# Top-k attention with two feed-forward layers: scores evicted over two PSUM banks at once for batch 0 and the batches made ahead

## The chip, the cores and the metric

One core of a Trainium2 chip runs the whole program. The metric is device time in microseconds (us). The kernel before was timed three times; the median is 1215.92 us.

## What is computed

The reference, cut to what matters (B, H, S, D are 4, 8, 576 and 64, top_k is 32, and x has 2304 rows of 512):

```python
scores = q @ k.transpose(0, 1, 3, 2) / np.sqrt(D)
kth = np.partition(scores, -top_k, axis=-1)[..., -top_k:-top_k + 1]
scores = np.where(scores >= kth, scores, -1e9)
attn = np.exp(scores - scores.max(-1, keepdims=True))
attn = attn / (attn.sum(-1, keepdims=True) + 1e-9)
x = (attn @ v).transpose(0, 2, 1, 3).reshape(B * S, H * D)
h = np.maximum(x @ w_in, 0.0)          # layer 1, d_ff = 2048
x = h * h @ w_out
h = x @ w2_in                          # layer 2
out = np.maximum(0.01 * h, h) @ w2_out
```

## The kernel before

**Tiles and pairs.** Attention is cut into 144 tiles of 128 rows of queries by 576 keys, in the order of `UNITS`: first the 36 tiles of batch 0 (tiles 0 to 35), then batch 1 and the rest. Two tiles make a pair; pairs 0 to 17 are batch 0. For each tile:

- `scores` multiplies on PE, in two halves of 288 keys (L279), each half into a PSUM bank of its own, and ACT copies each half to SBUF (L280). A tile takes 4 matmuls, or 8 where it crosses from one head to the other.
- DVE finds the 32 largest in each row: four MAX8 (L834) and three MATCH_REPLACE8 (L836), seven instructions a tile. The two tiles of a pair alternate, and the scheduler interleaves neighbouring pairs.
- POOL makes two constants of the pair from the maxima (`kf`, L291); ACT runs a Relu over each tile with them (L298), POOL subtracts (L299), ACT runs Exp with a row sum (L303), POOL and DVE make the reciprocal (L307, L308).
- PE transposes the tile (L317, L330), ACT evicts it to `PT` (L325, L343), PE multiplies by V (L401), DVE scales (`xn`, L432), and ACT and POOL split the result into a high and a low part (`xh` L433, `xl` L436), which is the input of the layers.

**Batches made ahead.** The scores of batches 2 and 3 (`EARLY`, 72 tiles) are made during pairs 0 to 15: matmul into tag `sp`, eviction to a `stage` tile, and a DMA to DRAM (`sd<-stage`, L283). They are read back when their turn comes (L287). Batch 0's scores go through tag `sd`, and batch 1's through the general banks `att`.

**PSUM until the layers start.** Three banks for `att`, two for `sd` (batch 0), three for `sp` (made ahead): eight. `sd` and `sp` rotate apart from each other. When the first block of 512 rows is ready, `open_mlp` gives their banks to the layers (`h`, one bank, and `acc`, four).

**The layers** run on PE in blocks (L580, L623, L625); ACT, DVE and POOL turn the weights into high and low parts (L513 to L526) and evict. The first block needs `xh` and `xl` of all four pairs of heads of its 512 rows. After that, work on the layers is interleaved with the attention of later pairs.

**What sets the order.** Each step is emitted at a slot (16 to a pair), and a scheduler then puts every engine's instructions into one fixed order, which is run strictly in that order. Tiles rotate through their buffers in the order of emission. Six score buffers (`s0` to `s5`, tile number modulo 6) and four `e` buffers are shared by all tiles.

Of the kernel before, what the change touches and what calls it, by code (L numbers as in the profile page):

```python
# [8 lines left out]
F = mybir.dt.float32  # L9
R = mybir.dt.float32r  # L10
U = mybir.dt.uint32
AF = mybir.ActivationFunctionType
# [31 lines left out]
FILL = (2, 245)  # L44
KPB = 2
NST = 3
SDB = 2
SPB = 3

NS = 6  # L50
NE = 4
# [20 lines left out]
def topk_attention_moe_moe2_kernel(  # L72
# [12 lines left out]
    P = 128  # L85
    DM, NF = 2 * NHP * D, w1.shape[0]
    NK = DM // P
    HALF = S // 2
# [5 lines left out]
    PE, ACT, DVE, POOL, SP = nc.tensor, nc.scalar, nc.vector, nc.gpsimd, nc.sync  # L94
# [6 lines left out]
    def bank():  # L101
        return psum.tile([P, 512], F, tag="att", name="att", bufs=3)
# [25 lines left out]
    for u in units:  # L128
        for hp in range(NHP):
            n = u["n"]  # L130
            uh = dict(u=u, hp=hp, n=n, b=u["b"], first=(u["t0"] == 0), ti=len(tiles), idx=len(uhs),
                      c0=P * (hp % 2) if n == 64 else 0)
# [14 lines left out]
    def direct(uh):  # L147
        return uh["b"] not in EARLY
# [10 lines left out]
    stage_psum = ahead_ctx.enter_context(tc.tile_pool(name="stage_psum", bufs=1, space=bass.MemoryType.PSUM))  # L159
    qsets = []  # L160
    for i in range(4):
        x = const if i < 2 else ahead
# [98 lines left out]
    def scores(t, half):  # L261
        uh = t["uh"]
        d = uh["qs"]
        kt = KT[uh["b"], uh["hp"]]
        if half == 0:
            if direct(uh):
                t["s"] = sbufs[t["i"] % NS]
            else:
                t["s"] = ahead.tile([P, S], F, tag="stage", name="stage", bufs=NST)
        ks = slice(half * HALF, (half + 1) * HALF)  # L270
        mm = [(x[:, h, c:c + P], kt[:, h, ks]) for h, c in t["parts"] for x in d]
        if not direct(uh):
            ps = stage_psum.tile([P, 512], F, tag="sp", name="sp", bufs=SPB)
        elif uh["b"] == 0:
            ps = stage_psum.tile([P, 512], F, tag="sd", name="sd", bufs=SDB)
        else:
            ps = bank()
        for i, (l, r) in enumerate(mm):
            PE.matmul(ps[:, 0:HALF], lhsT=l, rhs=r, start=i == 0, stop=i == len(mm) - 1)  # L279
        ACT.activation(t["s"][:, ks], ps[:, 0:HALF], AF.Copy)  # L280
        if half == 1 and not direct(uh):
            t["sd"] = dram.tile([P, S], F, tag=f"sd{t['i']}", name=f"sd{t['i']}")
            SP.dma_start(t["sd"], t["s"])  # L283
# [375 lines left out]
    for uh in uhs:  # L659
        b, hp, i = uh["b"], uh["hp"], uh.get("di")  # L660
# [50 lines left out]
    for n, key in enumerate(keys):  # L711
        ks = [(0, load_k, (*key, held[key]))]
        for h in range(2):
            ks.append((0, split_k, (*key, held[key], h)))
        if n == 0:
            fill += ks
        later = []
        for uh in later_uhs[key]:
            later += [(0, split_q, (uh, c)) for c in range(2)] + [(0, request, ())]
            for t in tiles[uh["ti"]:uh["last"] + 1]:  # L720
                later += [(1, scores, (t, half)) for half in range(2)]
        if n + 1 < len(keys):
            nk = keys[n + 1]
            ks = [(0, load_k, (*nk, held[nk]))]
            for h in range(2):
                ks.append((0, split_k, (*nk, held[nk], h)))
            m = len(later) // (len(ks) + 1)
            for x, item in enumerate(ks):
                later.insert((x + 1) * (m + 1) - 1, item)
        fill += later  # L730
# [9 lines left out]
    for p in range(NPAIRS):  # L740
        pr = dict(t=tiles[2 * p:2 * p + 2], p=p)
        pairs.append(pr)
        z = 16 * p
        for i, t in enumerate(pr["t"]):
            if direct(t["uh"]):
                at(z - DLEAD + 5 * i, scores, t, 0)
                at(z - DLEAD + 2 + 5 * i, scores, t, 1)
            else:
                at(z - LEAD + i, load_s, t)
            if i == 0:  # L750
                at(z + 14, shifts, pr)
            at(z + 14 + i, drop, pr, i)
            at(z + 16 + i, expo_sum, pr, i)
            if split(t["uh"]):
                at(z + 20 + i, norm, pr, i)
            at(max(z + 20 + 3 * i, z + 21 + i), pt_main, t)
        at(z + 18, recip, pr)
        at(z + 26, pt_left, pr)
# [60 lines left out]
    while slot <= last:  # L819
        p, i = divmod(slot, 16)  # L820
        if slot >= 0 and p < NPAIRS:
# [7 lines left out]
            x = i % 2  # L829
            t = pr["t"][x]  # L830
# [79 lines left out]
```

## Time and profile before

| | us |
|---|---|
| runs: lowest, median, highest | 1211.27, 1215.92, 1216.74 |
| span of the profiled execution | 1212.2 |
| PE busy | 1139.7 |
| DVE busy | 945.4 |
| ACT busy | 877.0 |
| POOL busy | 791.0 |

The span is 0.9 us above the lowest run and 3.7 below the median. The page gives no time outside the span, so the sum below is made on the span and then set on the median by those 3.7 us.

To read the views: a table by stretch gives, for each engine, busy time and, in brackets, the count of instructions in that stretch. In a timeline a row is start, duration, engine, line, operation, output<-input and count; where a row has x2, its duration covers both. The brackets at the end of a row are the time that the engine sat idle just before it, and who ended that.

### The profile page before, as it was taken

The page shows a single profiled execution, that of the slowest core. Times are in us where ns is not written, and L with a number is a line of the kernel's source. Part 1 is how long each engine was busy: PE and PEld are TensorE (multiplying, and loading weights), DVE is VectorE, ACT ScalarE, POOL GpSimd, SP SyncE. Part 2 cuts the span into 40 slices and gives each one's busy share as a digit, 9 for nine tenths or more (in the row PEclk, how much of TensorE's full clock was granted, in tenths as well). Part 3 has the DMA queues.
Part 4 walks back from the last instruction along what each step waited for, and adds up shares of the span by engine and source line. Part 5 has one row for each costly group of instructions (what it writes and reads, how often), then busy time and mean ns, then how long its engine had stood idle before and what let it go on. Part 6 is the DMA issues. An engine that isn't in the chain of part 4 may idle for free.

```text
span 1212.2 us, 20368 instructions
## 1 busy us (share of the span) xinstructions
PE 1139.7 (94%) x6388; PEld 994.3 (82%) x6388; DVE 945.4 (78%) x1944; ACT 877.0 (72%) x1939; POOL 791.0 (65%) x948
## 2 busy tenths in 40 slices
PE   5898878998899999999999999999999999999998
PEld 4676766886677879988998898788788899999997
DVE  7999999668888899999999999999999910110122
ACT  6889899888899997877767777676777763334322
POOL 7998977877889886667777685666576754004300
PEclk9899997999999999999999999999999999999999
DMA  9665656879889888889988788667576579779974
GB/s 308 230 226 194 196 196 245 268 252 315 306 292 343 296 279 272 301 289 367 349 294 286 256 280 285 202 229 233 193 232 223 197 261 374 255 254 339 359 251 137
DMA packets 110521, 323.24 MB, mean 267 GB/s; under 512 B 17488, under 2 KB 25680, under 8 KB 110416
## 3 DMA queue, kind: packets, MB, share of 16 engines
q1 hardware_dynamic: 107776, 317.24, 77.1%
q10 hardware_dynamic: 2640, 4.72, 1.1%
q8 instruction: 51, 0.84, 0.3%
q14 instruction: 54, 0.44, 0.1%
HBM read 254.54 MB, written 67.37 MB: 266 GB/s over the span
## 4 chain that ended last, share of the span: by engine, by line
PE 67%; ACT 10%; DVE 9%; DMA 3%; issue 2%; POOL 1%; ACTq 0%; SPq 0%; POOLq 0%
PE h L580 28%; PE acc L623 14%; PE acc L625 13%; DVE m L834 4%; PE att L412 3%; DVE w L836 3%; PE att L317 3%; DMA wraw<-in_w_dram 2%; PE att L401 2%; ACT e L303 2%; PE att L279 1%; ACT att L514 1%; ACT stage L280 1%; DVE PTs L323 1%; ACT s L280 1%
## 5 line engine op out<-in xcount | busy, mean ns | idle before, releaser
L580 PE MATMUL h<-xh,wi 128*128 128x512 f32 (+2 forms) x1280 | 350.0, 345 | 9.1 <-ACT wi L523 3.9
L834 DVE MAX8 m<-w 128x8 f32<-128x576 f32 x432 | 312.7, 748 | 1.5
L580 PEld LDWEIGHTS h<-xh,wi 128*128 128x128 f32 x1280 | 226.8, 190 | 38.6 <-ACT wi L523 4.3
L299 POOL TENSOR_TENSOR e<-s,e 128x576 f32<-128x576 f32 x144 | 203.4, 1431 | 26.6 <-ACT e L298 25.4
L836 DVE MATCH_REPLACE8 w<-m,w 128x576 f32<-128x576 f32 x288 | 213.2, 743 | 0.5
L580 PE MATMUL h<-xl,wi 128*128 128x512 f32 (+2 forms) x640 | 206.5, 340 | 1.4 <-DVE xl L637 1.1
L606 POOL TENSOR_TENSOR gl<-ga,gh 128x512 fp32r<-128x512 f32 (+2 forms) x160 | 162.8, 1017 | 38.1 <-ACT gh L605 32.5
L623 PE MATMUL acc<-gh,wo 128*128 128x512 f32 (+2 forms) x768 | 155.1, 340 | 0.0
L625 PE MATMUL acc<-wo,gh 128*128 128x512 f32 x576 | 151.5, 398 | 3.0 <-ACT gh L605 3.0
L603 POOL TENSOR_TENSOR ga<-ga,gb 128x512 f32<-128x512 f32 (+2 forms) x80 | 81.3, 1017 | 107.6 <-ACT gb L602 105.4
L623 PEld LDWEIGHTS acc<-gh,wo 128*128 128x128 f32 x768 | 125.9, 188 | 10.8 <-ACT gh L591 0.4
L580 PEld LDWEIGHTS h<-xl,wi 128*128 128x128 f32 x640 | 120.4, 189 | 14.7 <-DVE xl L637 4.0
L303 ACT ACTIVATE e<-e,kf 128x576 f32<-128x576 f32 x144 | 112.5, 782 | 17.3 <-POOL e L299 17.0
L625 PEld LDWEIGHTS acc<-wo,gh 128*128 128x128 f32 x576 | 103.9, 188 | 23.2 <-ACT gh L605 4.7
L298 ACT ACTIVATE e<-s,kf 128x576 f32<-128x576 f32 x144 | 105.7, 778 | 22.4 <-POOL kf L291 20.3
L834 DVE MAX8 m<-s 128x8 f32<-128x576 f32 x144 | 104.7, 748 | 13.4 <-ACT s L280 12.4
L592 POOL TENSOR_TENSOR ga<-ga 128x512 f32<-128x512 f32 (+2 forms) x80 | 66.2, 828 | 68.2 <-ACT gh L591 66.0
L836 DVE MATCH_REPLACE8 w<-m,s 128x576 f32<-128x576 f32 x144 | 107.0, 743 | 0.6
L317 PE MATMUL att<-ident,e 128*128 128x128 f32 x576 | 89.4, 284 | 13.0 <-ACT e L303 7.5
L312 ACT ACTIVATE e<-e,rc 128x576 f32<-128x576 f32 x108 | 78.0, 773 | 21.3 <-DVE rc L308 21.1
L317 PEld LDWEIGHTS att<-ident,e 128*128 128x128 f32 x576 | 69.8, 145 | 26.6 <-ACT e L303 12.8
L623 PE MATMUL acc<-gl,wo 128*128 128x512 f32 (+2 forms) x384 | 86.7, 345 | 0.2 <-POOL gl L606 0.2
(96 smaller groups left out, 2174.4 us busy)
## 6 DMA issues: line engine op xcount, KB each, us to landing
wi<-wd SPq DMA_DIRECT2D x160, 512.0 KB, 5.1
wo<-wd SPq DMA_DIRECT2D x160, 512.0 KB, 5.3
wraw<-in_w_dram SPq DMA_DIRECT2D x64, 512.0 KB, 5.6
sd<-stage SPq DMA_DIRECT2D x72, 288.0 KB, 2.8
s<-sd SPq DMA_DIRECT2D x72, 288.0 KB, 4.8
wd<-wi SPq DMA_DIRECT2D x32, 512.0 KB, 6.0
wd<-wo SPq DMA_DIRECT2D x32, 512.0 KB, 6.2
kraw<-in_k_dram SPq DMA_DIRECT2D x16, 576.0 KB, 4.3
```

Source lines behind the costliest of these rows:

```text
L298: ACT.activation(e, x, AF.Relu, bias=pr["kf"][:, i:i + 1], scale=-FAR)
L299: cur["pool"] = POOL.tensor_tensor(e, x, e, op=OP.subtract)
L303: ACT.activation(e, e, AF.Exp, bias=pr["nb"][:, i:i + 1], scale=0.125, accum_out=pr["sum"][:, i:i + 1])
L312: ACT.activation(e, e, AF.Copy, scale=pr["rc"][:, i:i + 1])
L317: PE.transpose(ps[:, j * P:(j + 1) * P], t["e"][:, j * P:(j + 1) * P], ident)
L580: PE.matmul(h[:, 0:n], lhsT=wi[:, w, c * P:(c + 1) * P], rhs=x[c][y][:, 0:n], start=cnt == 0, stop=cnt == 3 * NK - 1)
L603: POOL.tensor_tensor(a[:, 0:n], a[:, 0:n], b[:, 0:n], op=OP.subtract)
L606: (DVE if j >= GLD else POOL).tensor_tensor(gl[:, 0:n], a[:, 0:n], gh.bitcast(F)[:, 0:n], op=OP.subtract)
L623: PE.matmul(acc[c][:, 0:n], lhsT=wo[:, w, cs], rhs=g[:, 0:n], start=first, stop=last)
L625: PE.matmul(acc[c], lhsT=g[:, cs], rhs=wo[:, w, :], start=first, stop=last)
L834: cur["dve"] = DVE.max(out=m8[:, x, 8 * r:8 * r + 8], in_=t["s"] if r == 0 else t["w"])
L836: cur["dve"] = DVE.match_replace(out=t["w"], in_to_replace=m8[:, x, 8 * r:8 * r + 8], in_values=t["s"] if r == 0 else t["w"], imm_value=NEG)
```

## The change

For batch 0 and for the batches made ahead, the two halves of a tile go to one PSUM tile `ss` of two banks, and one ACT instruction evicts both halves (128x576) once the second half is done. `ss` has two buffers, four banks in all, shared by batch 0 and the batches made ahead; `sd` and `sp` are gone. Batch 1 keeps its two narrow evictions.

```diff
-SDB = 2
-SPB = 3
+SSB = 2
...
-        if not direct(uh):
-            ps = stage_psum.tile([P, 512], F, tag="sp", name="sp", bufs=SPB)
-        elif uh["b"] == 0:
-            ps = stage_psum.tile([P, 512], F, tag="sd", name="sd", bufs=SDB)
-        else:
-            ps = bank()
+        wide = not direct(uh) or uh["b"] == 0
+        if wide and half == 0:
+            t["ps"] = stage_psum.tile([P, 2, 512], F, tag="ss", name="ss", bufs=SSB)
+        ps = t["ps"][:, half] if wide else bank()
         for i, (l, r) in enumerate(mm):
             PE.matmul(ps[:, 0:HALF], lhsT=l, rhs=r, start=i == 0, stop=i == len(mm) - 1)
-        ACT.activation(t["s"][:, ks], ps[:, 0:HALF], AF.Copy)
+        if not wide:
+            ACT.activation(t["s"][:, ks], ps[:, 0:HALF], AF.Copy)
+        elif half == 1:
+            ACT.activation(t["s"].rearrange("p (x c) -> p x c", x=2), t.pop("ps")[:, :, 0:HALF], AF.Copy)
```

The scheduler answers with another order. In the rows below `s_104` to `s_109` are the score buffers s0 to s5, `e_110` to `e_113` the four `e` buffers, and a number after `m_` stands for one pair.

ACT before, around the scores of pair 9 (tiles 18 and 19, in `s_104` and `s_105`); the last two rows are the Relus of pair 7:

```order
L280 ACTIVATE s_104<-sd 128x288 x2
L280 ACTIVATE stage<-sp 128x288 x2
L303 ACTIVATE e_111,sum<-e_111,kf 128x576
L280 ACTIVATE stage<-sp 128x288
L366 ACTIVATE rb<-att 64x256
L325 ACTIVATE PT<-att 128x4x128
L280 ACTIVATE s_105<-sd 128x288
L116 ACTIVATE q_80<-qraw 128x256
L280 ACTIVATE s_105<-sd 128x288
L280 ACTIVATE stage<-sp 128x288
L298 ACTIVATE e_112<-s_106,kf 128x576
L298 ACTIVATE e_113<-s_107,kf 128x576
```

ACT now, at the same two tiles; the Relus here are those of pair 8:

```order
L280 ACTIVATE s_104<-ss 128x576
L325 ACTIVATE PT<-att 128x4x128 x2
L343 ACTIVATE PT<-att 64x256
L280 ACTIVATE stage<-ss 128x576
L298 ACTIVATE e_110<-s_108,kf 128x576
L298 ACTIVATE e_111<-s_109,kf 128x576
L115 ACTIVATE q_80<-qraw 128x256
L280 ACTIVATE s_105<-ss 128x576
```

Both tiles of pair 9 were evicted ahead of the Relus of pair 7. Now tile 18 stands ahead of those of pair 8, and tile 19 behind them: the evictions have moved one pair back.

DVE before, at the same place (`m_1328` is pair 8, `m_1471` pair 9):

```order
L834 MAX m_1471<-s_104 128x8
L308 RECIPROCAL rc<-sum 128x2
L834 MAX m_1328<-w 128x8
L432 TENSOR_TENSOR xn<-att,rb 128x256
L834 MAX m_1328<-w 128x8
L834 MAX m_1471<-s_105 128x8
L836 MATCH_REPLACE w<-m_1328,w 128x576 x2
L834 MAX m_1328<-w 128x8 x2
L836 MATCH_REPLACE w<-m_1471,s_104 128x576
L836 MATCH_REPLACE w<-m_1328,w 128x576
L834 MAX m_1471<-w 128x8
L834 MAX m_1328<-w 128x8
```

DVE now (`m_1213` is pair 8, `m_1342` pair 9):

```order
L836 MATCH_REPLACE w<-m_1213,w 128x576
L308 RECIPROCAL rc<-sum 128x2
L834 MAX m_1213<-w 128x8
L834 MAX m_1342<-s_104 128x8
L836 MATCH_REPLACE w<-m_1342,s_104 128x576
L834 MAX m_1342<-w 128x8
L836 MATCH_REPLACE w<-m_1342,w 128x576
L834 MAX m_1342<-w 128x8
L834 MAX m_1342<-s_105 128x8
```

DVE used to take both tiles of pair 9 well ahead of pair 8's last MAX. Now it takes the first right behind that MAX, and the second five instructions later.

ACT before, at the end of the stage: from the Relus of pair 17 to the last `xh` of the first block.

```order
L298 ACTIVATE e_112<-s_108,kf 128x576
L298 ACTIVATE e_113<-s_109,kf 128x576
L280 ACTIVATE s_106<-att 128x288
L366 ACTIVATE rb<-att 64x256
L514 ACTIVATE att<-wraw 128x512
L303 ACTIVATE e_112,sum<-e_112,kf 128x576
L280 ACTIVATE s_106<-att 128x288
L433 ACTIVATE xh_658<-xn 128x256
```

ACT now, at the same place:

```order
L298 ACTIVATE e_112<-s_108,kf 128x576
L298 ACTIVATE e_113<-s_109,kf 128x576
L278 ACTIVATE s_106<-att 128x288
L366 ACTIVATE rb<-att 64x256
L514 ACTIVATE att<-wraw 128x512
L303 ACTIVATE e_112,sum<-e_112,kf 128x576
L278 ACTIVATE s_106<-att 128x288
L433 ACTIVATE xh_607<-xn 128x256
```

Here nothing moved. Ahead of the eighth `xn` on DVE, which this `xh` reads, both orders hold 298 instructions, with the same count of each line; ahead of the `xh`, ACT has 108 fewer, all evictions of L280, and no other count differs.

## Rows read from the trace of the kernel before

**Rows 1.** The page: busy time, share of the span and instructions of each engine.

```profile
PE 1139.7 (94%) x6388; PEld 994.3 (82%) x6388; DVE 945.4 (78%) x1944; ACT 877.0 (72%) x1939; POOL 791.0 (65%) x948
```

**Rows 2.** Stretches: length, busy PE, PEld, DVE, ACT, POOL, clock, DMA share, GB/s.

```profile
9.10:30.00 20.90, 13.65 (x53) 11.63 (x54) 20.85 (x44) 14.16 (x34) 19.04 (x26) 0.91 1.09 330
30.00:100.00 70.00, 61.12 (x327) 48.90 (x325) 67.84 (x147) 61.40 (x167) 63.72 (x80) 0.90 0.68 225
100.00:150.00 50.00, 44.48 (x254) 35.19 (x254) 48.76 (x107) 44.10 (x126) 43.91 (x62) 1.00 0.61 197
150.00:200.00 50.00, 38.88 (x204) 31.17 (x203) 49.07 (x104) 47.45 (x122) 40.83 (x48) 0.86 0.65 224
```

**Rows 3.** The same table, once the layers run.

```profile
205.00:454.00 249.00, 235.85 (x1156) 191.51 (x1157) 206.14 (x391) 227.54 (x469) 210.38 (x210) 0.98 0.85 292
454.00:970.00 516.00, 504.09 (x2926) 448.38 (x2925) 509.76 (x1074) 383.97 (x807) 352.80 (x421) 1.00 0.78 264
970.00:1212.00 242.00, 236.52 (x1460) 224.11 (x1458) 35.81 (x68) 89.42 (x202) 52.33 (x72) 1.00 0.81 279
```

**Rows 4.** DVE's waits from 30 to 200 us: total, times, longest.

```profile
DVE rc L308 <- POOL sum L307: 1.2, 2, 0.7
DVE m L834 <- ACT s L280: 0.6, 1, 0.6
```

**Rows 5.** ACT's groups by form: busy, mean ns of one, idle before.

```profile
L280 ACT ACTIVATE stage<-sp 128x288 f32<-128x288 f32 x144 | 55.1, 433 | 8.5 <-PE sp L279 4.3 <-issue 3.1 <-PE sd L279 0.5
L280 ACT ACTIVATE s<-sd 128x288 f32<-128x288 f32 x72 | 29.2, 428 | 3.1 <-PE sd L279 3.0
L590 ACT ACTIVATE ga<-h 128x512 f32<-128x512 f32 x32 | 18.9, 591 | 10.1 <-PE h L580 10.1
L590 ACT ACTIVATE ga<-h 128x256 f32<-128x256 f32 x32 | 12.3, 383 | 27.6 <-PE h L580 27.3
```

**Rows 6.** Timeline, around pair 9's scores: ACT, then DVE.

```profile
88.03 1.45 ACT L298 ACTIVATE e<-s,kf 128x576 f32<-128x576 f32 x2
...
92.32 0.69 ACT L280 ACTIVATE s<-sd 128x288 f32<-128x288 f32 x2
...
96.18 0.41 ACT L280 ACTIVATE s<-sd 128x288 f32<-128x288 f32 x1
...
96.80 0.75 DVE L834 MAX8 m<-s 128x8 f32<-128x576 f32 x1
```

**Rows 7.** Timeline of pair 8: last MAX8 (the second of the two), POOL, Relus.

```profile
101.69 1.42 DVE L834 MAX8 m<-w 128x8 f32<-128x576 f32 x2
107.14 0.20 POOL L291 TENSOR_TENSOR kf<-m,scales 128x4 f32<-128x4 f32 x1
107.37 1.44 ACT L298 ACTIVATE e<-s,kf 128x576 f32<-128x576 f32 x2 [0.99 <-POOL kf L291]
```

**Rows 8.** Timeline of pair 3: last MAX8, then Relus.

```profile
49.32 0.74 DVE L834 MAX8 m<-w 128x8 f32<-128x576 f32 x1
...
57.26 1.48 ACT L298 ACTIVATE e<-s,kf 128x576 f32<-128x576 f32 x2
```

**Rows 9.** Timeline of pair 17, to the first block's layer.

```profile
198.48 1.41 DVE L834 MAX8 m<-w 128x8 f32<-128x576 f32 x2
200.46 0.20 POOL L291 TENSOR_TENSOR kf<-m,scales 128x4 f32<-128x4 f32 x1
200.69 1.44 ACT L298 ACTIVATE e<-s,kf 128x576 f32<-128x576 f32 x2 [0.57 <-POOL kf L291]
204.58 0.41 ACT L433 ACTIVATE xh<-xn 128x256 fp32r<-128x256 f32 x1
205.04 2.46 PE L580 MATMUL h<-xh,wi 128*128 128x512 f32 x5
```

**Rows 10.** Waits of weight loads on the evictions, whole span: total, times, longest.

```profile
PEld sp L279 <- ACT stage L280: 16.2, 21, 2.6
PEld sd L279 <- ACT s L280: 6.7, 15, 1.9
```

## Prediction

> **What bounds the kernel now.** I read the page first, then the table by stretch, then the waits, then the timeline at single tiles. The page alone [rows 1] would point at PE, busy for 94% of the span. But the change touches only instructions that end before 190 us, so the stage ahead of the layers counts. There the table [rows 2] shows DVE: of the 190.9 us from 9.1 to 200 it is busy 20.85 + 67.84 + 48.76 + 49.07 = 186.52 and idle 4.4. ACT is busy 167 of the same 190.9, POOL also 167, PE 158. So the stage lasts as long as DVE's seven instructions a tile. Afterwards [rows 3] PE carries the load from 205 to 454 (235.9 of 249) with ACT close behind, DVE and PE from 454 to 970 (509.8 and 504.1 of 516), and PE alone to the end. No stretch has room to take up a late start of the layers: PE is idle 13 us of 249, then 12 of 516, and its order there is fixed. I therefore take a shift of the layers' start as a shift of the end, one for one.
>
> **What starts the layers.** The last input of the first block is the eighth `xh`. Its chain [rows 9]: DVE ends pair 17's last MAX8 at 199.89, POOL makes the constants at 200.46, ACT's Relus follow at 200.69, `xh` at 204.58, and PE runs five matmuls of the layer from 205.04. The `order` rows at the end of the stage show the same instructions between Relus and `xh` in both kernels, and DVE's instructions ahead of it are the same 298. So those 4.4 us from the Relus on should stay, and the question is only when DVE is through with pair 17.
>
> **Part 1: fewer evictions on ACT.** Removed are 216 narrow evictions of 0.43 us each, added 108 wide ones [rows 5]. No 576-column copy out of PSUM is in the trace. From the rows of L590, 256 more columns cost 591 - 383 = 208 ns, so 64 more than 512 cost 52, and one wide eviction should take 0.64 us. Two narrow ones apart from each other take 0.86, two back to back 0.69 in all [rows 6]. A tile thus saves 0.05 to 0.22 us of ACT, 108 tiles 5 to 24; I take 12, nearer to the back-to-back row, as many are that. On the path this is worth almost nothing by itself, since DVE's 186.5 us are not touched. What it can give is idle time of DVE that it shortens: at most 4.4 us, of which 0.6 us is put down to an eviction and 1.2 to sums that wait behind Exp [rows 4]. I take a gain of 1.5 here, bounds 0 and 4.4. One instruction of pair 18 less stands ahead of pair 17's last MAX8 on DVE, which is 0.7 at most and lies within that bound.
>
> **Part 2: the eviction waits for the whole tile.** Half a tile's matmuls no longer hide under the other half's eviction. At the very first tile DVE starts 0.64 - 0.43 = 0.2 us later. Later tiles carry this in part 3.
>
> **Part 3: batch 0 shares its banks.** Before, batch 0 had two banks to itself and its scores ran ahead of what batches 2 and 3 did in theirs. Now all tiles take turns in two buffers, so a tile of batch 0 waits until the tile two turns earlier has been evicted, whichever batch it is of. PE already waited 16.2 and 6.7 us for evictions in this stage [rows 10]; transposes queue behind such a wait on PE. The order shows what the scheduler makes of it: evictions of batch 0 have moved one pair back on ACT. Before, those of pair p stood ahead of the Relus of pair p-2, now ahead of or among those of pair p-1. ACT runs in order, and a Relu can't start before DVE has finished its pair and POOL has made the constants. So the eviction of a tile is now tied to a DVE pair that ends shortly before DVE needs this tile.
>
> *The room of a tile.* Take tile 19. ACT now evicts it behind the Relus of pair 8, one copy of `q` in between: 1.45 + 0.42 + 0.64 = 2.5 us, or 2.2 with what overlaps. DVE takes it five instructions after pair 8's last MAX8, at about 0.69 us each (two MAX8 take 1.42 [rows 7]), so 3.4 later. Relus may thus start 3.4 - 2.2 = 1.2 us after that MAX8 before DVE waits. I call 1.2 the room. In the trace of before, the Relus of pair 8 started at 107.37, and the MAX8 ended at 103.11 [rows 7]: a lag of 4.3. With that lag DVE would wait 3 us for tile 19. Before, the same tile's second half was evicted at 96.59 and taken at 96.80 [rows 6], behind the Relus of pair 6, so it just came in time as well, but with no such tie to pair 8.
>
> *All tiles.* The same working for tiles 4 to 35, from both orders and the durations of the trace, gives a room of 2.7 to 10.6 us before, the middle one 6.8, and of 0.9 to 8.1 now, the middle one 2.9. The lag, read the same way for pairs 0 to 17, goes from 0.8 us at pair 17 [rows 9] to 7.2 at pair 3 [rows 8], mean 3.9. Where the lag is over the room DVE waits. With a lag of 3.9 for every pair the waits of pairs 2 to 17 sum to 21 us now, with 3.0 to 11, with 2.0 to 4. The same sum for before at 3.9 gives 2.3, where the trace shows 0.6 [rows 4], so it counts too high. It must: a wait of DVE lets POOL and ACT catch up, which shortens the next lag. I take the lag as 3.0, less than the 3.9 of before since ACT has 12 us less to do in this stage, and half of the sum: 5.5 us. Bounds 0 and 21.
>
> **The sum.** 5.5 of waits, 0.2 at the start, less the gain of 1.5: 4.2 us. On the span 1212.2 + 4.2 = 1216.4; on the median, 3.7 higher, 1220. About 0.5%, some 6 us, is what a measurement of this kernel can tell from no change, so 1220 is no change that counts, with the weight on the slower side.
>
> **Rivals.**
> Slower: the waits of DVE, the same mechanism at the lag of before. Speaking for it: POOL, not only ACT, makes the lag (of pair 8's 4.3 us, 4.0 passed until POOL came to the constants at 107.14 [rows 7]), and POOL loses no work. Against it: DVE's idle time before is only 4.4 us at that lag. With 10 to 20 us of waits the median is 1224 to 1234. It decides from a lag of a little over 3 us, where half of the sum passes 6.
>
> Nothing: the lag shrinks as far as the room, DVE waits no more than before, and the time is 1212 to 1217.
>
> Faster: DVE's 4.4 us go and the layers start at 200.6; that gives 1211.5, still within 0.5%. To be faster by more, something after 205 has to gain too, for instance the weights' conversions on ACT (227.5 busy of 249 [rows 3]); but the count of them ahead of the last `xh` is the same in both orders, and no eviction of that stage is changed. That would be some 1207.
>
> By the Trainium skill, "Perfetto Trace Analysis", section "Optimizing Scalar/DVE Operations", larger operations improve throughput if the engine is saturated, and if ScalarE isn't, but causes bubbles on others, breaking instructions up may let work be done sooner. ACT is busy 167 of 190.9 us here, so by the second half of that rule this change goes the wrong way, to the time of the slower rival; no row of before shows which half holds.
>
> **How the numbers follow.** My forecast of a small loss, 1217 to 1222, has 0.30; nothing, 1212 to 1217, 0.23: these two make the 0.53 for within 0.5%. Slower by more 0.38, faster by more 0.09. The range leaves out the faster end and the uppermost part of the slower one: 1210 to 1234. It also holds the spread of the three runs, 5.5 us.
>
> **What would show it.** Right: DVE's waits for L280 between 30 and 200 us rise from 0.6 to some 5 us, one per pair and mostly at a tile's first MAX8; the first block's `xh` comes at 207 to 210; from there on, each stretch is as long as before, and the distance from `xh` to the end stays at 1007 us. Wide evictions of 0.62 to 0.68 us, and ACT busy about 12 us less before 200, check part 1. The forecast is wrong if `xh` comes before 203, if DVE idles over 15 us in this stage, or if the end moves by several us more or less than `xh` does: then the order after 205, which also differs in places, or the banks handed over to the layers, has its own effect.

## The result and the profile after

The changed kernel takes 1230.05 us (median of four runs, 1225.04 to 1234.42), beside 1214.53 for the kernel before on the same chip. The ratio is 1.0131, with a 95% interval of 1.0101 to 1.0162. The change makes the kernel some 16 us slower. The profiled execution has a span of 1229.8 us, 17.6 more than before.

The views that answer to the rows above follow. First the page's busy times (as rows 1):

```profile
PE 1145.9 (93%) x6388; PEld 1003.7 (82%) x6388; DVE 948.2 (77%) x1944; ACT 872.2 (71%) x1831; POOL 791.4 (64%) x948
```

ACT lost its 108 instructions. By form (as rows 5), a wide eviction takes 0.65 us, where the prediction had 0.64:

```profile
L280 ACT ACTIVATE stage<-ss 128x576 f32<-128x576 f32 x72 | 45.9, 651 | 13.9 <-issue 4.1 <-DMA sd<-stage 3.5 <-PE ss L276 3.1
L280 ACT ACTIVATE s<-ss 128x576 f32<-128x576 f32 x36 | 23.1, 645 | 3.4 <-PE ss L276 3.0
```

These 69.0 us stand where 84.3 stood [rows 5]; ACT as a whole is busy 4.8 us less. The saving is real, and it is not on the path. The stage ahead of the layers, in the stretches of rows 2 (length, then busy PE, PEld, DVE, ACT, POOL, then granted clock, DMA share, GB/s). The last line ends some 0.7 us behind pair 17's last MAX8, which ends at 209.16 (the first of the two that begin at 208.41 in the timeline below):

```profile
9.10:30.00 20.90, 11.98 (x43) 9.40 (x42) 19.77 (x41) 12.47 (x24) 18.49 (x25) 1.00 1.08 331
30.00:100.00 70.00, 57.56 (x314) 46.38 (x312) 65.95 (x142) 58.22 (x120) 63.17 (x80) 0.95 0.65 218
100.00:150.00 50.00, 44.65 (x246) 36.51 (x247) 46.41 (x98) 42.11 (x90) 40.62 (x57) 0.93 0.55 187
150.00:200.00 50.00, 37.72 (x210) 30.59 (x208) 46.77 (x99) 42.93 (x93) 36.02 (x47) 0.93 0.61 210
...
9.10:209.82 200.72, 158.97 (x828) 127.55 (x827) 188.72 (x399) 162.21 (x338) 165.45 (x212) 0.93 0.66 221
```

The same stretch of the kernel before, which ends as far behind its own last MAX8 of pair 17 (199.89 us):

```profile
9.10:200.56 191.46, 158.69 (x836) 127.40 (x836) 187.08 (x399) 167.23 (x445) 167.91 (x215) 0.92 0.70 229
```

Both hold 399 instructions of DVE. The stretch is 9.3 us longer: DVE's idle time went from 191.46 - 187.08 = 4.4 to 200.72 - 188.72 = 12.0 us, and its instructions took 1.6 longer. DVE's waits from 30 to 200 us (as rows 4: total, times, longest) say for whom it idled:

```profile
DVE m L834 <- ACT s L280: 5.9, 9, 1.5
DVE rc L308 <- POOL sum L307: 1.9, 2, 1.6
DVE xn L432 <- ACT rb L366: 1.6, 2, 0.8
```

The waits for evictions of scores went from 0.6 to 5.9 us. The first tile adds some more. DVE's first MAX8 starts at 10.13 us, where it started at 9.12.

From there to the layers, the timeline that answers to rows 9 (start, duration, engine, line, operation, output<-input, count, and in brackets the idle time just before with who ended it):

```profile
204.22 8.48 PE L401 MATMUL att<-PT,VN 128*128 128x256 f32 x18
...
208.41 1.41 DVE L834 MAX8 m<-w 128x8 f32<-128x576 f32 x2
...
209.12 1.26 ACT L115 ACTIVATE KT<-kraw 128x576 fp32r<-128x576 f32 x2 [3.26 <-DMA kraw<-in_k_dram]
...
209.94 2.78 POOL L240 TENSOR_TENSOR KT<-kraw,KT 64x576 fp32r<-64x576 f32 x2 [2.47 <-ACT KT L115]
...
212.80 0.20 POOL L291 TENSOR_TENSOR kf<-m,scales 128x4 f32<-128x4 f32 x1
...
213.03 1.44 ACT L298 ACTIVATE e<-s,kf 128x576 f32<-128x576 f32 x2 [2.09 <-POOL kf L291]
...
214.79 0.38 ACT L366 ACTIVATE rb<-att 64x256 f32<-64x256 f32 x1
...
215.20 0.42 DVE L432 TENSOR_TENSOR xn<-att,rb 128x256 f32<-128x256 f32 x1 [1.88 <-ACT rb L366]
...
216.92 0.41 ACT L433 ACTIVATE xh<-xn 128x256 fp32r<-128x256 f32 x1
```

Before, POOL made pair 17's constants 0.6 us after the end of the last MAX8 [rows 9]. Now it comes to them 3.6 us after it, because it first waits for the last K of batch 1 (`KT`: ACT copies the high part, POOL makes the low part from it). ACT copies this K at 209.12, as soon as its load has landed. The last K of batch 1 was copied at 190.44 before. So the eighth `xh` comes 12.3 us later (216.92 for 204.58): 9.3 from DVE and 3.1 from this K. From this `xh` to the end it is 1012.9 us, where it was 1007.6. The last 5.3 us are lost there, in one execution of each kernel.

### The profile page after: what moved, and what is told of

The parts are those of the page before. It is cut to its first block, busy times and chain, and to the rows that moved or that the text cites. A ratio compares the mean times of both kernels' runs of the same rounds, so it can differ in the third digit from the quotient of the medians.

```text
span 1229.8 us, 20233 instructions
## 1 busy us (share of the span) xinstructions
PE 1145.9 (93%) x6388; PEld 1003.7 (82%) x6388; DVE 948.2 (77%) x1944; ACT 872.2 (71%) x1831; POOL 791.4 (64%) x948
## 4 chain that ended last, share of the span: by engine, by line
PE 62%; POOL 10%; ACT 10%; DVE 9%; issue 4%; DMA 4%; POOLq 0%; ACTq 0%; SPq 0%; DVEq 0%
PE h L580 25%; PE acc L625 12%; PE acc L623 12%; DVE m L834 4%; PE att L317 3%; DVE w L836 3%; PE att L412 3%; PE ss L276 3%; POOL e L299 2%; PE att L401 2%; ACT e L298 1%; ACT e L303 1%; POOL q L257 1%; POOL KTa L240 1%; DMA wraw<-in_w_dram 1%
## 5 line engine op out<-in xcount | busy, mean ns | idle before, releaser
L623 PE MATMUL acc<-gh,wo 128*128 128x512 f32 (+2 forms) x768 | 159.1, 345 | 1.1 <-ACT gh L591 1.1
L276 PE MATMUL ss<-KTa,q 128*128 128x288 f32 x320 | 64.1, 337 | 22.1 <-ACT stage L280 9.3
```

Of the source, the lines that this page charges most:

```text
L623: PE.matmul(acc[c][:, 0:n], lhsT=wo[:, w, cs], rhs=g[:, 0:n], start=first, stop=last)
```

## The experiments

Ratios are against runs of the kernel before on the same chip. "xh" is the start of the first block's eighth `xh`, 204.58 us before, read like all places in time from one profiled execution of each kernel. Line numbers differ by a few between the kernels. "Waits" are DVE's waits for the evictions of scores from 30 to 200 us, 0.6 us before. The expectations speak of four theories: DVE waits because batch 0 shares its rotation (1), the wide eviction itself costs (2), a part is lost behind the layers' start (3), and the batches made ahead lack the fifth bank (4).

### Scores issued earlier, 42 slots

In the changed kernel, and as a control in the kernel before:

```diff
-DLEAD = 30
+DLEAD = 42
```

> The changed kernel with one number changed: the scheduler issues direct scores 42 slots ahead instead of 30, so the wide evictions of batch 0 come earlier on ACT (room of a tile: middle 14.0 us instead of 3.2, smallest 7.2 instead of 1.0). Shared rotation, wide evictions and banks stay. Theory 1 (DVE waits, because the shared rotation moves batch 0's evictions behind the Relus of the pair before): DVE's waits for L280 between 30 and 205 us fall from 5.9 us to under 1, the last xh of the first block comes at 203 to 208 us instead of 216.9, and the time at 1212 to 1220. Theory 2 (the wide eviction itself costs, since it waits for both halves of a tile): time stays at 1226 to 1232. Theory 3 (part of the loss lies behind the layers' start): xh at 203 to 208, but time 1217 to 1224, since xh to the end stays longer than before's 1007 us by some 5.

> Control: the kernel before with the same change of lead, 30 to 42 slots; narrow evictions and tags of their own. Room of a tile: middle 19.7 us. Its DVE waits for L280 were 0.6 us, so there is nothing to win: theory 1 expects 1209 to 1217, the same as before within 0.5%. If it gains as much as the changed kernel does with this lead, then the lead helps by something else than those waits, and theory 1 is not shown by the first run. Theories 2 and 3 say nothing else of it.

Measured: 1249.20 us, ratio 1.0267 (1.0240 to 1.0295), and 1244.98 us, ratio 1.0235 (1.0210 to 1.0260). DVE's waits for scores are gone, as theory 1 expected, but both kernels are slower still. The choice of 42 was a mistake of mine. Six score buffers are three pairs. With 42 slots the scores of pair p+3 are issued at slot 16p + 6, ahead of the Relus of pair p (16p + 14), which read the same buffers. So these Relus read, and wait for, scores that come three pairs later. They then follow the last MAX8 of their pair by 9.9 and some 7.5 us on average, and by over 18 us at pair 17. This part of the computation is changed, and the two runs tell nothing about the change.

### Scores issued earlier, 38 slots and seven buffers

With seven buffers the tile that takes a buffer over is issued behind the Relu that reads it.

```diff
-NS = 6
+NS = 7
...
-DLEAD = 30
+DLEAD = 38
```

> The changed kernel with seven score buffers instead of six, which lets the direct scores be issued 38 slots ahead instead of 30 without writing over a tile that its Relu hasn't read. Shared rotation, wide evictions and the four banks stay. Room of a tile: middle 5.6 us instead of 3.2; waits at a lag of 3.0 sum to 4.4 us instead of 10.9. Theory 1 (DVE waits for batch 0's evictions, which the shared rotation puts late on ACT): DVE's waits for L280 between 30 and 205 us at most 3 instead of 5.9, last xh of the first block at 207 to 212 us instead of 216.9, time 1218 to 1225. Theory 2 (the wide eviction itself) and theory 4 (four banks instead of five slow down the batches made ahead, and with them batch 1's K and the layers' start): time stays at 1226 to 1233.

> Control: the kernel before with the same two numbers changed (seven score buffers, 38 slots). All theories: within 0.5% of before, 1210 to 1221, since its DVE hardly waits for L280. If it gains or loses more than that, the run of the changed kernel with these numbers has to be read against this one.

Measured: 1221.54 us, ratio 1.0059 (1.0034 to 1.0083), for the changed kernel, and 1220.70 us, ratio 1.0050 (1.0027 to 1.0072), for the control. The two numbers themselves cost 0.5%, and on top of them the change costs 1221.54 / 1220.70 = 1.0007, which is nothing that could be measured. `xh` comes at 211.14 and 211.53. DVE's waits in the changed kernel and in the control, from 30 to 200 us:

```profile
DVE m L834 <- ACT s L280: 3.9, 5, 1.7
```

```profile
DVE m L834 <- ACT s L280: 0.4, 1, 0.4
```

So beside its control the change loses nothing when the scores are issued earlier. The control's own `xh` is 7 us later than before, though, and what holds it there may hide some of the change's loss; no run tells. The waits fell by a third only, short of the half that theory 1 had expected, and `xh` is on time within the expected 207 to 212. The lead also brings the last K forward: it is copied at 195.67 instead of 209.12. The run doesn't separate the two effects.

### Which part costs: width, sharing, banks

Wide evictions as in the change, in rotations of their own (one buffer of two banks each):

```diff
-            t["ps"] = stage_psum.tile([P, 2, 512], F, tag="ss", name="ss", bufs=SSB)
+            tag = "sd" if direct(uh) else "sp"
+            t["ps"] = stage_psum.tile([P, 2, 512], F, tag=tag, name=tag, bufs=1)
```

> Wide evictions as in the change, but batch 0 and the batches made ahead each keep a PSUM buffer of two banks of their own (one buffer each, the same four banks as the change, not shared). Room of a tile: middle 7.4 us, smallest 1.9. Theory 1 (the sharing ties batch 0 to the batches made ahead): DVE's waits for L280 under 2 us, xh at 203 to 208, time 1211 to 1219. Theory 2 (the wide eviction itself): with one buffer each a tile's matmuls can't start before the eviction of the tile before, so it is no better than the change, 1226 to 1234. Theory 3: xh as by theory 1, time 1217 to 1224.

Measured: 1240.59 us, ratio 1.0199 (1.0173 to 1.0224). This is slower than the change, and theory 1 is wrong on it: `xh` 210.32, and hardly a wait (0.2 us). The loss is elsewhere. With one buffer the batches made ahead go tile by tile between PE and ACT. PE waits 20.1 us for `stage` from 30 to 205 us (14.3 in the change, 11.0 before). Their last eviction comes at 239.72 us, and the layers' first matmuls, whose PSUM takes over these banks, come only behind it:

```profile
239.72 0.65 ACT L281 ACTIVATE stage<-sp 128x576 f32<-128x576 f32 x1 [1.16 <-issue]
```

```profile
240.43 3.78 PE L581 MATMUL h<-xh,wi 128*128 128x512 f32 x8 [0.31 <-ACT stage L281]
```

That eviction was at 189.59 us before, and is at 193.04 in the change, and in both the layers went on from the eighth `xh`. Here the inputs are ready at 210.32 and the layers stand still for 30 us, until the banks are free. From `xh` to the end this kernel takes 1029.8 us, 22 more than before; from 240.43 to the end it takes 999.7, where it was 1007.2 from 205.04 on [rows 9]. So the whole loss lies ahead of the layers' start.

The two shared buffers of the change, but each half evicted by itself:

```diff
-        if not wide:
-            ACT.activation(t["s"][:, ks], ps[:, 0:HALF], AF.Copy)
-        elif half == 1:
-            ACT.activation(t["s"].rearrange("p (x c) -> p x c", x=2), t.pop("ps")[:, :, 0:HALF], AF.Copy)
+        ACT.activation(t["s"][:, ks], ps[:, 0:HALF], AF.Copy)
```

> The changed kernel with the two shared two-bank buffers, but each half evicted by a narrow instruction of its own, as before. Room of a tile by the orders: middle 0.1 us, smallest -3.5, so the tie is closer still than in the change. Theory 1: DVE waits far more than in the change, 15 to 40 us for L280 between 30 and 205, xh at 225 to 250, time 1238 to 1265. Theory 2 (the wide eviction is what costs): without it the time goes back to 1211 to 1220. Theory 3: as theory 1 up to xh, and some 5 us more from there.

Measured: 1263.70 us, ratio 1.0394 (1.0368 to 1.0420), `xh` 249.72. DVE's waits from 30 to 200 us:

```profile
DVE m L831 <- ACT s L277: 16.3, 14, 4.5
```

This is what theory 1 expected, and against theory 2. Without the wide eviction, in the same banks, the loss is three times as large.

Only batch 0 wide, from a buffer of two banks of its own, with the batches made ahead as before (against the kernel before; cut, batch 0's eviction is that of the change):

```diff
-        elif uh["b"] == 0:
-            ps = stage_psum.tile([P, 512], F, tag="sd", name="sd", bufs=SDB)
+        wide = uh["b"] == 0
+        if wide and half == 0:
+            t["ps"] = stage_psum.tile([P, 2, 512], F, tag="sd", name="sd", bufs=1)
```

> Only batch 0 is evicted wide, from one PSUM buffer of two banks of its own; the batches made ahead keep their three banks and narrow evictions. Nothing is shared, five banks as before. Room of a tile: middle 7.2 us. Theory 1 (sharing) and theory 4 (a bank less for the batches made ahead): 1211 to 1219, xh at 203 to 208. Theory 2 (the wide eviction itself, since a tile's matmuls wait for the eviction of the whole tile before): 1222 to 1232, with PE's waits for s of L280 of 10 us and more ahead of 205.

Measured: 1218.40 us, ratio 1.0023 (1.0010 to 1.0036), `xh` 206.61, waits 0.4 us. Theory 2 would have had 1222 or more.

Only the sharing: narrow evictions in one rotation of five banks.

```diff
-        if not direct(uh):
-            ps = stage_psum.tile([P, 512], F, tag="sp", name="sp", bufs=SPB)
-        elif uh["b"] == 0:
-            ps = stage_psum.tile([P, 512], F, tag="sd", name="sd", bufs=SDB)
+        if not direct(uh) or uh["b"] == 0:
+            ps = stage_psum.tile([P, 512], F, tag="ss", name="ss", bufs=SDB + SPB)
```

> Only the sharing: all narrow evictions as before, five banks as before, but in one rotation of five for batch 0 and the batches made ahead. Room of a tile: middle 5.6 us, waits at a lag of 3.0 sum to 4.7 us (the change: 3.2 and 10.9). Theory 1: something like half of the change's loss, 1218 to 1226, DVE's waits for L280 of 2 to 6 us between 30 and 205. Theories 2 and 4 (neither a wide eviction nor a bank less): 1211 to 1218.

Measured: 1227.22 us, ratio 1.0105 (1.0073 to 1.0136).

```profile
DVE m L832 <- ACT s L278: 3.2, 3, 1.6
```

The waits are as theory 1 expected, the time is 1 us above its range. But only a part comes by its way: `xh` is at 208.12, 3.5 us late, and another 11.7 us are lost behind it (1019.3 us from `xh` to the end). So sharing does cost by itself. Theory 1 accounts for a quarter of that, and the rest falls to theory 3, where no cause was tested.

Only the bank: the kernel before with two banks for the batches made ahead.

```diff
-SPB = 3
+SPB = 2
```

> The kernel before with two instead of three banks for the batches made ahead: four banks in all, as in the change, but narrow evictions and rotations of their own. Theory 1 (sharing): batch 0 isn't touched, room of a tile in the middle 7.1 us, so DVE's waits for L280 stay under 2 us, xh at 203 to 208, time 1212 to 1220. Theory 4 (a bank less for the batches made ahead): more waits of PE for stage (over 25 us between 30 and 205 instead of 11), the last stage eviction after 195 instead of 189 us, time 1222 to 1232.

Measured: 1236.28 us, ratio 1.0174 (1.0154 to 1.0194). Theory 4 is borne out in the last eviction and more than borne out in the time, and theory 1 falls on this run. A bank less costs more than the whole change does, with narrow evictions and nothing shared. PE waits 19.1 us for `stage` from 30 to 205 (expected: over 25). The last eviction for the batches made ahead, and DVE's waits from 30 to 200 us:

```profile
229.11 0.47 ACT L280 ACTIVATE stage<-sp 128x288 f32<-128x288 f32 x1
```

```profile
DVE m L834 <- ACT s L280: 5.5, 5, 1.7
```

DVE waits for scores here as much as in the change, although batch 0 has its own two banks. The longest of these waits, ahead of 66.52 us, shows one way:

```profile
64.01 0.71 ACT L280 ACTIVATE stage<-sp 128x288 f32<-128x288 f32 x2 [3.74 <-DMA sd<-stage]
...
65.72 0.71 ACT L280 ACTIVATE s<-sd 128x288 f32<-128x288 f32 x2
```

PE had finished these scores by 55.6 us. Their eviction stood on ACT behind evictions of the batches made ahead, and ACT waited there for a `stage` tile to be written to DRAM. The wait ahead of 132.70 us (0.9) has the same form. From 30 to 205 us ACT waits 8.7 us for such writes, 3.5 in the change and none before. So banks apart don't make queues apart, and here the queue was ACT's. PE's waits for `stage` don't explain it alone: with both streams wide and apart they were as long (20.1 us), and DVE waited 0.2. The last scores of batch 0 are evicted at 191.70 us, 14 later than before, and `xh` is at 224.76. Here too the layers begin only behind the last eviction above, at 229.98, and take 1005.6 us from there.

Wide evictions in rotations of their own once more, with two buffers for the batches made ahead. The two banks come from the one that the change leaves free and from a general one, so the control is the kernel before with two general banks. Both have this line; the wide kernel also has the tags of the first run of this section, with two buffers for `sp`:

```diff
-        return psum.tile([P, 512], F, tag="att", name="att", bufs=3)
+        return psum.tile([P, 512], F, tag="att", name="att", bufs=2)
```

> Wide evictions for batch 0 and the batches made ahead, each in a rotation of its own: one buffer of two banks for batch 0, two for the batches made ahead, paid for with one general bank (att 2 instead of 3). Room of a tile: middle 7.3 us. To be read against the control with two general banks. Theory 1 (the sharing costs, not the wide eviction): within 0.5% of the control, DVE's waits for L280 between 30 and 205 us under 2.5, batch 1's last K copied ahead of pair 16's Relus, before 195 us. Theory 2 (the wide eviction costs): 1% or more slower than the control, with PE's waits for s and stage above those of the control by 10 us.

> Control of the run above: the kernel before with two general banks instead of three, nothing else. No theory here says what a general bank is worth; P, PV products, batch 1's scores and the weights' conversions go through them, so a loss of 0 to 2% (1215 to 1240) is expected. It serves for the difference.

Measured: 1283.20 us, ratio 1.0572 (1.0548 to 1.0595), and for the control 1287.62 us, ratio 1.0604 (1.0582 to 1.0626). A general bank is worth 6%, three times the most that I had put down. With it gone from both, wide evictions of all these tiles are 1283.20 / 1287.62 = 0.997 of the control, no loss. Waits for batch 0's evictions are 1.1 us in the wide kernel, beside a single one of 2.6 for a narrow eviction of batch 1, and 1.1 for all in the control. `xh` is at 212.38 and 212.08. The batches made ahead finish 19 us sooner than in the control (169.29 for 188.60), without a gain that the intervals can tell from none. This holds where the general banks limit the kernel. What it would be with three of them can't be tried, since nine banks would be needed.

### The late K

The changed kernel with batch 1's last K copied behind the Relus of pair 17. On every engine the order is the same up to that place.

```diff
-        split_hi(kt, raw, st["i"] in HI_SET)
+        with behind("relu") if (b, hp) == (1, 3) else ExitStack():
+            split_hi(kt, raw, st["i"] in HI_SET)
```

Here `relu` is the last Relu issued, up to pair 17's.

> The changed kernel with one step moved: the copies of batch 1's last K on ACT (KT), which waited 3.3 us for their load at 209.1 us just ahead of pair 17's Relus, are put behind these Relus. Nothing else moves ahead of them. If this wait holds the layers' start on top of DVE's lateness: pair 17's Relus follow its last MAX8 (209.2) by 1 us instead of 3.9, rb is then held by PE's product with V (213.3), and the last xh of the first block comes at 215 to 216 us instead of 216.9; time 1227 to 1230. If the late K alone were the cause of the change's loss: xh at 204 to 209, time 1214 to 1222. If it only hides behind PE: xh at 216.5 to 217.5, time unchanged.

Measured: 1224.47 us, ratio 1.0084 (1.0069 to 1.0099). The end of the stage:

```profile
203.83 5.73 PE L403 MATMUL att<-PT,VN 128*128 128x256 f32 x18
...
208.72 0.20 POOL L292 TENSOR_TENSOR kf<-m,scales 128x4 f32<-128x4 f32 x1 [1.64 <-DVE m L836]
208.95 1.44 ACT L299 ACTIVATE e<-s,kf 128x576 f32<-128x576 f32 x2 [1.16 <-POOL kf L292]
...
210.30 1.24 ACT L115 ACTIVATE KT<-kraw 128x576 fp32r<-128x576 f32 x2
211.86 0.38 ACT L368 ACTIVATE rb<-att 64x256 f32<-64x256 f32 x1
...
214.77 0.41 ACT L435 ACTIVATE xh<-xn 128x256 fp32r<-128x256 f32 x1
```

The wait for K held `xh`. POOL now makes pair 17's constants right behind the last MAX8, and `xh` comes at 214.77 instead of 216.92. That is a little more than expected, because PE's product with V was faster too (5.73 for 8.48 us). Of the delay that is left, 10.2 us, 8.3 stand ahead of the Relus, where DVE is late (208.95 for 200.69). The other 1.9 come behind them, 1.2 of it because the K's copies now stand between the Relus and `rb`, so the move gives back less than the wait that it takes away. From `xh` to the end it is 1007.7 us, as before (1007.6): the other 5.3 us of the change are gone as well. PE's order behind the first layer's start also differs between the two kernels, and the granted clock from `xh` to the end was 0.99, as before, where the change had 0.98. So what brought them back stays open.

### All of it in one table

| banks, rotation, eviction | ratio | waits | last `s` of batch 0 (start) | last `stage` (start) | xh | xh to the end |
|---|---|---|---|---|---|---|
| 5, apart, narrow (before) | 1 | 0.6 | 177.8 | 189.6 | 204.6 | 1007.6 |
| 5, apart, batch 0 wide | 1.0023 | 0.4 | 180.2 | 193.1 | 206.6 | 1009.5 |
| 5, shared, narrow | 1.0105 | 3.2 | 182.6 | 179.9 | 208.1 | 1019.3 |
| 4, shared, wide (the change) | 1.0131 | 5.9 | 196.2 | 193.0 | 216.9 | 1012.9 |
| 4, apart, narrow | 1.0174 | 5.5 | 191.7 | 229.1 | 224.8 | 1010.8 |
| 4, apart, wide | 1.0199 | 0.2 | 179.1 | 239.7 | 210.3 | 1029.8 |
| 4, shared, narrow halves | 1.0394 | 16.3 | 230.8 | 225.2 | 249.7 | 1012.4 |

**Width.** With five banks, apart, it costs next to nothing for batch 0. With four, apart, the intervals of wide and narrow overlap (1.0199 and 1.0174).

**Sharing** makes DVE wait, as the pairs of rows that differ in it show: 0.2 and 5.9 us (four banks, wide), 0.6 and 3.2 (five, narrow), 5.5 and 16.3 (four, narrow, where the shared buffers also hold both halves of a tile). It doesn't always cost time. Among the wide kernels with four banks the shared rotation is the better one (1.0131 against 1.0199, the intervals don't touch), since apart the batches made ahead finish so late that the layers wait for their banks.

**Banks.** With four banks each of these kernels loses 1.3% or more, whatever its width or rotation, and one of the two streams is late: batch 0, or the batches made ahead, or both. With the scores issued earlier (38 slots, seven buffers) the four banks cost nothing beside the control. I read this so: the change pays for its wide evictions with a bank, and the sharing decides which stream pays. This is argued from the rows, not shown: each row is also an order of its own. In the three slowest rows with four banks the granted clock up to `xh` was lower too (0.83, 0.86 and 0.85, from the top), where it was 0.92 before and in the change; no run separates that.

## Why the prediction was right, and where it was not

**The outcome.** 1230 lies in the range of 1210 to 1234, but the likeliest case, 1217 to 1222, didn't come. The rival "slower" did, at 1224 to 1234, though with a smaller wait than it named and two losses that it didn't. So it is partly luck that the range holds it: the upper end was meant for waits of up to 20 us, and they rose by 5.3. One of the prediction's own signs of being wrong also came, an end that moves by several us more than `xh` does (17.6 for 12.3).

**What bounds the kernel** held. DVE is the busiest engine of the stage, and the layers start behind it.

**Part 1** held in the price of the instruction, 0.65 us for 0.64 forecast. The saving of 12 us on ACT did not. From 9.1 to 200 ACT is busy 155.7 us, 11.4 less, but that is luck: the changed kernel has got less far by then. Up to pair 17's last MAX8, in the two lines on that stretch, ACT is busy 162.2 us for 167.2. That is 5.0 less, the lower end of the 5 to 24, as if every tile had been evicted back to back before. The gain of 1.5 us didn't come. DVE's other waits, for sums and for `rb`, didn't fall either: the sums' went from 1.2 us [rows 4] to 1.9.

**Part 2** said 0.2 us for the first tile. It was 1.0 (10.13 for 9.12). With batch 0's banks apart the first MAX8 comes at 9.07 and 9.18 us, wide, and with the shared rotation at 9.87, narrow. So it goes with the shared rotation, not with the width.

**Part 3, the waits**, was the term that the prediction doubted most, and it came out as sized. The lag is 2.9 us on average, where 3.0 was taken, and the waits rose by 5.9 - 0.6 = 5.3 us, where 5.5 was taken. The mechanism is there too: 9 short waits, the longest 1.5 us. The cause that the prediction gave, the sharing, is borne out by the pairs of rows above, 0.2 and 5.9 us for the change's own banks and width. It isn't the only possible one: with four banks apart, narrow, DVE waits 5.5 us with nothing shared.

**The step that failed** is the one ahead of part 1: that "the question is only when DVE is through with pair 17". The 4.4 us from the Relus on did stay (213.03 to 217.38), but the Relus came 3.9 us after DVE's last MAX8, where it had been 0.8. I had read the order from pair 17's Relus on, and there nothing moved. I hadn't read what stands just ahead of them on ACT and POOL. Batch 1's last K stood ahead of the Relus of pair 16 and moved behind them, ahead of those of pair 17. Batch 1's four K's come one behind the other through one load buffer, and each takes over the buffer of a K of batch 0 (L200, four buffers), whose last scores are now evicted at 196.2 instead of 177.8 us. The first of the four is copied at 178.6 us instead of 158.8, the last at 209.1 instead of 190.4. The load of the last was issued at 203.84, just as POOL had finished with the third in the one load buffer (201.03 + 2.79). It cost 3.1 us between DVE's end and POOL's constants, and moving it gave 2.2 back at `xh`.

**One for one**, the shift from `xh` to the end, was off by 5.3 us (1012.9 for 1007). The prediction had named the order behind 205 us, and the banks handed over to the layers, as what could do this. The banks did it in the two runs with four banks apart, where the layers waited for them, and not in the change. Over the runs with three general banks, those with 42 slots left aside, the distance is 1007.6 to 1019.3, and 1029.8 where the layers wait for their banks. No run separates what makes this spread. One candidate is the order behind 205 us, which the scheduler writes anew for every kernel. The other, which the prediction didn't name, is TensorE's granted clock. From `xh` to the end it was 0.99 before and 0.98 in the change (columns as in rows 2):

```profile
204.58:1212.20 1007.62, 976.78 (x5539) 864.00 (x5537) 752.13 (x1532) 701.35 (x1478) 615.51 (x701) 0.99 0.80 274
216.92:1229.80 1012.88, 979.97 (x5537) 870.77 (x5537) 752.12 (x1532) 701.16 (x1478) 615.44 (x701) 0.98 0.80 273
```

PE is busy 3.2 us longer there and idle 2.1 us more, while DVE, ACT and POOL do the same work in the same time. The four executions of the changed kernel, all in one order, took 1223.3, 1226.7, 1229.8 and 1232.6 us at a mean granted clock of 0.977, 0.974, 0.972 and 0.968. So 5.3 us between two single executions is less than one order spreads by itself. A forecast for this kernel should have had some 10 us of width for it, and mine had none.

**What the sum left out** is the bank. The section on the change says that four banks take the place of `sd` and `sp`, which had two and three. The prediction priced the rotation, but never the fifth bank: with `sp` cut from three banks to two alone, the loss is 1.7%. The row for it was there, PE's 16.2 us of waits for `stage` evictions [rows 10]. I used it for the sharing alone. By the Trainium skill, "Perfetto Trace Analysis", section "Matmul Optimizations", all eight PSUM banks should be in use. The change uses seven, and the run with `sp` cut, also seven, agrees with the rule (1.0174). Eight in use are not enough by themselves: with one general bank fewer and four for the batches made ahead the loss was 5.7%.

**The rule on larger operations**, from the same page, section "Optimizing Scalar/DVE Operations", had been set beside the slower rival. The runs don't bear out its second half. In banks of its own a wide eviction costs 0.2% for batch 0 and nothing for all tiles beside the control; in shared buffers it is the narrow halves that lose more. By these runs it is not the size of the instruction alone that made the change slow.

## What to carry to other kernels

A larger eviction has to be charged with the buffers it takes, not only with its own time: name the bank that is given up, and price it by a row of the producer's waits for that tag, before the instruction is priced at all. Where two streams share an engine that runs in order, separate banks need not keep a wait of one from the other (here ACT's, for a write to DRAM). Where banks are handed on to a later stage, the last user of them sets when that stage can start. Where a stream comes later, look for everything that can only start behind its end (here the next batch's K, which takes its buffers over), and read the order of every engine on the path from its last undisturbed instruction on, not from the first one of interest.

## What the runs showed of the hardware that I had not expected

The products with V at the end of the stage cost 5.35 us before and 8.48 after, for the same 18 matmuls. The table by stretch (columns as above, the granted clock third from the end) has a clock of 0.84 for these products in the kernel before:

```profile
195.40:200.80 5.40, 5.38 (x20) 4.16 (x21) 5.40 (x14) 3.92 (x10) 5.09 (x7) 0.84 0.60 237
```

In the changed kernel, first the stretch ahead of the products, then the products. There the clock is 0.50, the lower level of 1.2 GHz, from the first to the last:

```profile
195.60:204.20 8.60, 4.24 (x23) 3.12 (x23) 8.60 (x19) 8.54 (x20) 7.38 (x8) 0.90 0.64 203
204.20:212.70 8.50, 8.50 (x21) 5.94 (x20) 8.50 (x21) 3.40 (x7) 5.87 (x6) 0.50 0.56 196
```

Ahead of it PE had been busy for 4.24 of 8.60 us, at a granted 0.90. With the K moved, PE had been busy for 4.01 of 8.20 us ahead of the same products, and there the clock came back within them:

```profile
203.80:209.20 5.40, 5.40 (x20) 4.02 (x19) 5.40 (x11) 2.52 (x6) 3.32 (x5) 0.76 0.82 297
```

So much the same idle time ahead gave 8.5 us in one execution and 5.7 in the other. In the changed kernel this didn't set the end, since ACT came to `rb` at 214.79, 0.8 us after PE's last product (213.28 + 0.70). What in the activity ahead made the difference no run tells.
